# An attention and two-MLP kernel on one core: pieces of the written opening put in another order, zero products by a table

## The chip, the cores and the metric

The program runs on one core of a Trainium2 chip. The metric is device time in microseconds (us) of one execution; of several runs the median counts. The profile is one profiled execution. Its engines are PE (TensorE, matrix products; PEld is its weight load), DVE (VectorE), ACT (ScalarE), POOL (GpSimd) and SP (SyncE, which issues most DMAs). Every engine carries out its instructions in the order in which they are written.

## The reference, cut to what matters

Three layers follow one another on 4 x 768 = 3072 tokens of width 512: chunked attention with 8 heads and 8 memory keys, then an MLP with softplus, then an MLP with a leaky ReLU.

```python
attn_out = _attn_ref(q, k, v, mem_k, mem_v)         # chunks of 32, context 16 left, 8 right
x = attn_out.transpose(0, 2, 1, 3).reshape(3072, 512)
h = x @ moe_w_in                                    # 512 x 2048
x = (maximum(h, 0) + log1p(exp(-abs(h)))) @ moe_w_out
h = x @ moe2_w_in
return (maximum(h, 0) + alpha * minimum(h, 0)) @ moe2_w_out
```

The weights come as 64-bit floats, which the kernel turns into 32-bit ones by integer operations on DVE.

## The kernel before, in words

**Tiles.** Attention works on 24 tiles t of 128 tokens (4 make a block of 512). The first MLP runs over steps i = (block b, column group f of 128): `h.i` is PE's twelve products of x with the first weights, `out.i` the twelve products of the result with the second weights, summed over f in four banks of a block. Every operand is split in a high and a low part (three products instead of one). SEGMENTS begins with (block 0, f 0 to 3), (block 1, f 0 to 3), (block 0, f 4 to 7), (block 1, f 4 to 7): steps h.0 to h.3, h.4 to h.7, and so on, so h.4 to h.7 use the weights of h.0 to h.3 again. The second MLP follows in `pairs`, which the change does not touch.

**Pieces.** The opening and the first MLP are cut into pieces, added in `schedule`. Names used below:
- loads, issued by SP and moved by the DMA: `qk.t` (three DMAs: two halves of the queries, then the keys), `v.t` (six DMAs), `cst`, and `raw.n`, the n-th weight half of 128 x 512 64-bit words (`load_raw`). The halves k come in the order 0, 2, 1, 4, 3, 6, 5, 8, 7, ...; an even k = 2f is the first weight of f, an odd k its second.
- per weight half, on DVE: `ab` (`magnitude`), `cl` (`clamp`), `ca`, `cb`, `cv` (`convert_a` to `convert_c`); `wh` on ACT and `wl` on POOL split it in high and low.
- per attention tile: `qz` (POOL; DVE for tile 0) clears the half of the query tile that stays zero, `qo` and `qp` (ACT) place the queries, `km` (POOL) the memory keys; `s` (PE) scores, `m` and `c` (DVE) maximum and subtraction, `e` (ACT) exp, `n` and `r` (DVE) sum and reciprocal, `w` (POOL) the product with it, `t` (PE) transposes, `pt` (ACT) copies them, `v*` (PE) the values, `xh` (ACT) and `xl` (DVE) the split into x.
- per step: `h` (PE), `sp` (ACT softplus), `hi` (ACT), `lo` (DVE), `out` (PE). After the last step of a segment `dr` copies the four banks and `dd` stores them.

**Order.** `Plan.run` simulates the pieces greedily, with assumed durations and due times from the table O, eight times over, and the plan with the earliest end is taken; its `order` is then written out piece by piece. `InOrder` (line 71 is its call in the profile, so all rows have that line) ties each engine's instructions to that order. Rooms limit it: three raw buffers (`rpool`), three words, sixteen weight or tile rooms (`wpool`), two buffers each of ta and g.

**Zero products.** `keep_busy(name, ps)` writes `spare[name]` products with a zero operand ahead of a piece, into the bank that the piece then overwrites. Before, `spare` follows from the waits that the plan itself expects:

```python
    for name, (since, until) in plan.idle.items():
        if since > 0.0:
            spare[name] = max(0, int((until - since - 0.5) * 0.6 / 0.22))
        else:
            spare[name] = 8 + int((until - since - 7.0) * 0.6 / 0.22)
    for piece in plan.order:
        piece[4]()
```

By this the kernel before has 11 ahead of s.0, 9 of s.1, 2 of t.0, 3 each of t.1, v\*.1, v\*.2 and t.7, 4 each of v\*.3 and v\*.6, and 1 of t.5.

Of the kernel before, what the change touches and what calls it, by code (L numbers as in the profile page):

```python
# [81 lines left out]
PLAN = []  # L82
RUNS = 8
O = {'qo': 19.43, 'km': 103.61, 's': 132.4, 'm': 86.98, 'c': -51.87, 'e': 175.6, 'n': -19.49, 'r': -46.35, 'w': -19.52, 't': 95.77, 'pt': 85.42, 'v': 4.11, 'xh': -85.13, 'xl': -37.52, 'first': 4.43, 'gap': 13.49, 'second': 13.8, 'gap2': 10.89, 'raw': 76.14, 'ab': -97.97, 'cl': -24.77, 'ca': -41.63, 'cb': -28.14, 'cc': -52.39, 'wh': 1.69, 'wl': -37.29, 'odd': 61.8, 'sp': 29.0, 'hi': -84.66, 'lo': 120.66, 'out': 14.22, 'wait': 0.06, 'sloads': 10.35, 'qo0': 31.77, 'qo1': 59.63, 'km0': 45.44, 'km1': -1.09, 's0': 33.53, 's1': 68.06, 'm0': 99.26, 'm1': -29.86, 'c0': 87.42, 'c1': 86.99, 'e0': -47.46, 'e1': 46.23, 'n0': 20.17, 'n1': -4.91, 'r0': 23.19, 'r1': -6.49, 'w0': -81.15, 'w1': -23.28, 't0': 107.79, 't1': -40.96, 'pt0': 0.74, 'pt1': -5.53, 'v0': -87.68, 'v1': 71.52, 'xh0': -18.53, 'xh1': -22.32, 'xl0': 2.53, 'xl1': 34.49, 'by0': 3.34, 'by1': 1.01, 'va': -80.0, 'vb': -248.8, 'vc': -188.24, 'vd': -121.62, 'ra': -92.44, 'rb': -99.39, 'rc': -59.46, 'wld': -3.93, 'dra': -16.84, 'qpd': -4.87, 'ca0': 0.43, 'ca1': -2.85}


class Plan:
# [9 lines left out]
    def add(self, name, engine, us, due, work, after=(), take=(), give=(), table=None):  # L97
        assert name not in self.pieces, name
        self.pieces[name] = (engine, us, due, work, after, take, give, table)
# [4 lines left out]
    def run(self):  # L104
# [10 lines left out]
        while left:  # L115
# [19 lines left out]
            if engine and engine != "DMA":  # L135
                near = [x for x in able if x[3] == engine and x[0] < t + O["wait"]]
                if engine == "PE" and self.beside(last_pe):
# [39 lines left out]
def attention_mlp_mlp_kernel(ctx: ExitStack, tc, qk, v, w1, w2, consts, out):  # L177
# [19 lines left out]
    pe, act, dve, pool, sp = (InOrder(tc, e) for e in (nc.tensor, nc.scalar, nc.vector, nc.gpsimd, nc.sync))  # L197
# [19 lines left out]
    def load_raw(layer, k):  # L217

        t = rpool.tile([P, DM], mybir.dt.uint64, tag="raw", name="raw")
        sp.dma_start(out=t, in_=(w1, w2)[layer][k // 2, k % 2])  # L220
        raws[layer, k] = t.bitcast(I32).rearrange("p (n two) -> p n two", two=2)

    def magnitude(layer, k):
        m = words[layer, k] = tpool.tile([P, DM], F32, tag="word", name="word", bufs=3)
        dve.tensor_scalar(
            out=m.bitcast(I32), in0=raws[layer, k][:, :, 1], scalar1=1, scalar2=1,
            op0=ALU.logical_shift_left, op1=ALU.logical_shift_right,
        )

    def clamp(layer, k, eng=None):  # L230
        m = words[layer, k]
        (eng or pool).tensor_scalar(out=m, in0=m, scalar1=DBL_LEAST, scalar2=DBL_MOST, op0=ALU.max, op1=ALU.min)
# [7 lines left out]
    def convert_a(layer, k):  # L240
        mi = words[layer, k].bitcast(I32)
        dve.tensor_scalar(
            out=mi, in0=mi, scalar1=3, scalar2=0x3FFFFFFF,
            op0=ALU.logical_shift_left, op1=ALU.bitwise_and,
        )

    def convert_b(layer, k):
        r, mi = raws[layer, k], words[layer, k].bitcast(I32)
        dve.scalar_tensor_tensor(
            out=mi, in0=r[:, :, 1], scalar=-0x40000000, in1=mi, op0=ALU.bitwise_and, op1=ALU.bitwise_or  # L250
        )
# [56 lines left out]
    pt = [tpool.tile([P, NPAIR, 2, D], F32, tag=tag, name="pt") for tag in ("tb", "tl")]  # L308
# [598 lines left out]
    def schedule(when):  # L907
# [8 lines left out]
        def dma(name, issue, move, due, work, after=(), take=(), give=(), eng="SP"):  # L916
            add(("i",) + name, eng, issue, due, work, after, take)
            add(("x",) + name, "DMA", move, due, nothing, [("i",) + name])
            add(name, "", 2.0, due, nothing, [("x",) + name], [], give)

        for n, k in enumerate(order):
            f = k // 2
            need = when[first_use[f]] + (O["odd"] if k % 2 else 0)
            dma(("raw", n), 0.45, 1.9, (O["ra"], O["rb"], O["rc"])[n] if n < 3 else need - O["raw"], lambda k=k: load_raw(0, k), [("i", "raw", n - 1)] if n else [("i", "qk", TB - 1, 2)], ["raw"])
            add(("ab", n), "DVE", 0.45, need - O["ab"], lambda k=k: magnitude(0, k), [("raw", n)] + ([("ab", n - 1)] if n else []), ["word"])
            add(("cl", n), "DVE", 0.46, need - O["cl"], lambda k=k: clamp(0, k, dve), [("ab", n)])
            add(("ca", n), "DVE", 0.47, need - O["ca"], lambda k=k: convert_a(0, k), [("cl", n)] + ([("cv", n - 1)] if n else []))
            add(("cb", n), "DVE", 0.71, need - O["cb"], lambda k=k: convert_b(0, k), [("ca", n)])
# [175 lines left out]
        when = came + [came[-1] + 2.72 * 2]  # L1104
    plan = min(plans, key=lambda x: x.done["out", last - 1])

    for name, (since, until) in plan.idle.items():
        if since > 0.0:
            spare[name] = max(0, int((until - since - 0.5) * 0.6 / 0.22))
        else:  # L1110
            spare[name] = 8 + int((until - since - 7.0) * 0.6 / 0.22)
# [69 lines left out]
```

## Time and profile before

| | |
|---|---|
| runs shown | 1091.04 us median of 3 (1089.97 to 1093.57) |
| the profiled execution's own time | 1090.53 us |
| its span, first to last instruction | 1088.6 us |
| PE busy | 1064.7 us (98%) |
| DVE busy | 715.6 us (66%) |
| ACT busy | 559.0 us (51%) |
| POOL busy | 231.2 us (21%) |

The time is 1.9 us more than the span. Busy shares are means over the whole span; the opening, some 7% of it, looks different from the rest. Matmul records overlap by about 0.15 us and a few are missing, so lengths of groups are taken from start to start.

### The profile page before, as it was taken

How to read it: one execution, taken by the hardware profiler on the slowest of the kernel's cores; microseconds unless marked ns; L12 is line 12 of the kernel's file. 1: busy time of each engine (PE TensorE's matmuls, PEld its weight loads, DVE VectorE, ACT ScalarE, POOL GpSimd, SP SyncE). 2: the span in 40 equal slices, each digit the busy share in tenths (PEclk: the TensorE clock that was granted, in tenths of full speed). 3: DMA queues.
4: the chain of work that ended last, by engine and by line, in shares of the span. 5: the costliest groups of instructions: out<-in, count | busy, mean ns of one | idle time of the engine just before them, and what ended most of it. 6: DMA issues, size and time to landing. Idle time of an engine off the chain costs nothing.

```text
span 1088.6 us, 16448 instructions
## 1 busy us (share of the span) xinstructions
PE 1064.7 (98%) x5999; PEld 873.6 (80%) x6003; DVE 715.6 (66%) x1150; ACT 559.0 (51%) x974; POOL 231.2 (21%) x281
## 2 busy tenths in 40 slices
PE   6789999999999999999999999999999999999998
PEld 4578878888888888888888888888888888888886
DVE  6789989566744554454358156678666779566976
ACT  5654335565553554353244355664555755456643
POOL 4434434334222332223233400000000000000000
PEclk9999999999999999999999999999999999999999
DMA  9955574658644565444356373799874999856904
GB/s 227 226 154 173 170 190 129 172 170 207 173 143 155 158 188 139 171 123 145 107 201 229 132 289 125 283 280 323 199 278 174 329 299 256 251 209 251 377 1 78
DMA packets 173840, 214.55 MB, mean 197 GB/s; under 512 B 96064, under 2 KB 125888, under 8 KB 166848
## 3 DMA queue, kind: packets, MB, share of 16 engines
q1 hardware_dynamic: 169456, 196.59, 56.7%
q0 software_dynamic: 4032, 16.78, 7.8%
q8 instruction: 48, 0.79, 0.3%
q14 instruction: 32, 0.26, 0.1%
q10 hardware_dynamic: 272, 0.13, 0.0%
HBM read 154.74 MB, written 46.14 MB: 185 GB/s over the span
## 4 chain that ended last, share of the span: by engine, by line
PE 91%; DVE 3%; DMA 2%; issue 1%; SPq 1%; ACT 1%; POOL 0%; DVEq 0%; ACTq 0%; POOLq 0%
PE ps_q L71 42%; PE ps_o L71 23%; PE ps_hh L71 22%; DVE word L71 2%; PE ps_x L71 2%; PE ps_s L71 2%; DMA raw<-in_w_dram 1%; PE ps_t L71 1%; DMA qk<-in_qk_dram 1%; SPq L71 1%; DMA v<-in_v_dram 0%; ACT pt L71 0%; DVE sm L71 0%; DVE o_sb L71 0%; DVE g L71 0%
## 5 line engine op out<-in xcount | busy, mean ns | idle before, releaser
L71 PE MATMUL ps_hh<-x,wsplit 128*128 128x512 f32 x1152 | 281.1, 393 | 0.3 <-DVE x L71 0.2
L71 PE MATMUL ps_o<-g,wsplit 128*128 128x512 f32 x1152 | 279.1, 391 | 0.8 <-ACT ta L71 0.7
L71 PEld LDWEIGHTS ps_o<-g,wsplit 128*128 128x128 f32 x1152 | 214.8, 188 | 46.5 <-ACT ta L71 1.1
L71 PEld LDWEIGHTS ps_hh<-x,wsplit 128*128 128x128 f32 x1152 | 215.3, 189 | 45.5 <-DVE x L71 0.5
L71 PE MATMUL ps_q<-g,wout 128*128 128x512 f32 x1008 | 229.3, 389 | 0.0
L71 PE MATMUL ps_q<-xop,win 128*128 128x512 f32 x1008 | 229.1, 389 | 0.0
L71 PEld LDWEIGHTS ps_q<-g,wout 128*128 128x128 f32 x1008 | 189.0, 188 | 39.8 <-ACT gb L71 0.5
L71 PEld LDWEIGHTS ps_q<-xop,win 128*128 128x128 f32 x1008 | 189.2, 188 | 39.3
L71 DVE TENSOR_TENSOR g<-ta,g 128x512 fp32r<-128x512 f32 x96 | 71.2, 742 | 132.0 <-ACT g L71 131.8
L71 ACT CAST g<-gb 128x512 fp32r<-128x512 f32 x168 | 100.9, 622 | 89.6 <-PE ps_q L71 64.2
L71 DVE TENSOR_TENSOR g<-gb,g 128x512 fp32r<-128x512 f32 x168 | 114.0, 686 | 35.5 <-ACT g L71 33.6
L71 ACT CAST g<-ta 128x512 fp32r<-128x512 f32 x96 | 59.6, 621 | 147.5 <-PE ps_o L71 147.3
L71 ACT ACTIVATE ta<-ps_hh 128x512 f32<-128x512 f32 x96 | 57.4, 598 | 106.4 <-PE ps_hh L71 106.0
L71 DVE SCALAR_TENSOR_TENSOR word<-raw,word 128x512 int32<-128x512 int32 x128 | 104.6, 818 | 2.5
L71 ACT ACTIVATE tp<-gb 128x512 f32<-128x512 f32 x48 | 30.4, 633 | 91.8 <-DVE gb L71 91.8
L71 POOL TENSOR_TENSOR wst<-wsum,wst 128x512 fp32r<-128x512 f32 x32 | 42.1, 1316 | 122.4 <-ACT wst L71 122.3
L71 DVE TENSOR_SCALAR word<-word 128x512 f32<-128x512 f32 (+1 forms) x128 | 66.1, 521 | 1.8
L71 POOL DMA_DIRECT2D gb<-gb x12 | 10.5, 872 | 264.2 <-DVE g L71 183.0
L71 POOL TENSOR_TENSOR wsplit<-word,wsplit 128x512 fp32r<-128x512 f32 x32 | 48.9, 1530 | 64.4 <-ACT wsplit L71 64.2
L71 DVE TENSOR_SCALAR word<-raw 128x512 int32<-128x512 int32 x64 | 38.1, 597 | 36.8 <-DMA raw<-in_w_dram 23.8
L71 DVE SCALAR_TENSOR_TENSOR gb<-gb,tp 128x512 f32<-128x512 f32 x48 | 33.2, 691 | 44.0 <-ACT tp L71 44.0
L71 POOL TENSOR_TENSOR wst<-word,wst 128x512 fp32r<-128x512 f32 (+1 forms) x32 | 36.6, 1145 | 113.4 <-ACT wst L71 113.4
(81 smaller groups left out, 926.0 us busy)
## 6 DMA issues: line engine op xcount, KB each, us to landing
wout<-out_ops SPq DMA_DIRECT2D x42, 1024.0 KB
raw<-in_w_dram SPq DMA_DIRECT2D x64, 512.0 KB
win<-in_ops SPq DMA_DIRECT2D x24, 1024.0 KB
win<-in_ops SPq DMA_DIRECT2D x24, 768.0 KB
out_ops<-wst SPq DMA_DIRECT2D x56, 256.0 KB
in_ops<-wst SPq DMA_DIRECT2D x24, 512.0 KB
gb<-gb POOLq DMA_DIRECT2D x12, 1024.0 KB, 13.3
v<-in_v_dram SPq DMA_DIRECT2D x48, 128.0 KB
```

Source lines behind the costliest of these rows:

```text
L71: i = getattr(self.engine, name)(*args, **kw)
```

## The change

A table LATER of 293 pairs is added. After the plan is chosen, each pair (name, other) takes the piece `name` out of the order and puts it back right behind `other`. A second table WAITS replaces the plan's own waits as the source of the zero products. Nothing that is computed changes.

```diff
+LATER = ((('i', 'qk', 1, 2), 'qzero'), (('x', 'qk', 0, 2), ('x', 'qk', 1, 2)), (('qo', 0), ('qp', 1)), (('qp', 0), ('qo', 0)), (('i', 'v', 0), ('i', 'raw', 2)), (('i', 'v', 1), ('i', 'v', 0)),
...
+(('qz', 7), ('vr', 7)), (('qz', 2), ('qz', 7)), (('qz', 3), ('qz', 2)), (('qz', 6), ('qz', 3)), (('qz', 5), ('qz', 6)), (('qz', 4), ('qz', 5)), (('km', 0), ('qz', 4)), (('s', 0), ('km', 0)),
...
+(('i', 'v', 5), ('i', 'raw', 5)), (('x', 'qk', 4, 2), ('x', 'raw', 4)), (('qk', 4, 2), ('x', 'qk', 4, 2)), (('km', 4), ('qk', 4, 2)), (('i', 'qk', 6, 2), ('i', 'raw', 6)),
...
+(('raw', 7), ('qk', 7, 2)), (('ab', 6), ('raw', 7)), (('cl', 5), ('ab', 6)), (('m', 4), ('cl', 5)), (('c', 4), ('ca', 5)), (('cl', 6), ('c', 4)), (('wh', 3), ('cb', 5)), (('e', 4), ('wh', 3)), (('sp', 0), ('e', 4)),
...
+(('hi', 10), ('hi', 11)), (('lo', 11), ('hi', 10)), (('lo', 10), ('lo', 11)), (('out', 10), ('lo', 10)), (('sp', 12), ('out', 10)))
+
+WAITS = {('s', 0): (0.0, 9.7), ('s', 3): (13.6, 14.8), ('t', 0): (15.9, 16.5), ('t', 1): (17.2, 19.0), ('v*', 0): (19.7, 21.8), ('v*', 1): (24.9, 26.8), ('v*', 3): (28.2, 30.0), ('s', 4): (32.9, 35.8), ('v*', 7): (70.2, 70.3)}
...
     plan = min(plans, key=lambda x: x.done["out", last - 1])
 
-    for name, (since, until) in plan.idle.items():
+    for name, other in LATER:
+        names = [piece[3] for piece in plan.order]
+        piece = plan.order.pop(names.index(name))
+        names.remove(name)
+        plan.order.insert(names.index(other) + 1, piece)
+    for name, (since, until) in WAITS.items():
         if since > 0.0:
             spare[name] = max(0, int((until - since - 0.5) * 0.6 / 0.22))
         else:
```

Carried out on the plan's order, the pairs give these orders per engine (the part that differs and that is spoken of; what follows is as before).

PE before: s.0 s.1 t.0 s.2 v\*.0 s.3 t.1 v\*.1 t.2 v\*.2 t.3 v\*.3 s.4 h.0 s.5 h.1 t.4 s.6 v\*.4 out.0 s.7 t.5 h.2 v\*.5 t.6 v\*.6 t.7 h.3 v\*.7 out.1 h.4 out.2 h.5 out.3, and so on in turn.
PE after: s.0 s.1 s.2 s.3 t.0 t.1 v\*.0 t.2 t.3 v\*.1 v\*.3 v\*.2 s.4 h.0 h.1 t.4 out.0 v\*.4 s.5 out.1 s.6 h.2 s.7 t.5 h.3 t.6 v\*.5 out.2 v\*.6 t.7 v\*.7 out.3 h.4 h.5 h.6 out.4 h.7 h.8 out.5 h.9 out.6 h.10 out.7 h.11 out.8 out.9.

DVE before, from m.4: m.4 cv.2 c.4 ab.3 n.4 cl.3 r.4 ca.3 m.5 cb.3 c.5 cv.3 lo.0 m.6 lo.1 c.6 ab.4 n.5 cl.4 r.5 n.6 ca.4 r.6 xl.4 m.7 cb.4 c.7 ab.5 cv.4 cl.5 n.7 ca.5 r.7 cb.5 ab.6.
DVE after, from ab.3: ab.3 cv.2 xl.1 cl.3 ca.3 cb.3 cv.3 ab.4 cl.4 xl.2 ca.4 cb.4 cv.4 xl.3 ab.5 ab.6 cl.5 m.4 ca.5 c.4 cl.6 cb.5 n.4 r.4 ab.7 cv.5 lo.0 cl.7 ca.6 cb.6 cv.6 ca.7 cb.7 cv.7 lo.1 m.5 c.5 xl.4 m.6 n.5 c.6 r.5 n.6 m.7 r.6 c.7 lo.2 ab.8 ab.9.

ACT after, from wh.4: wh.4 qo.4 qp.4 wh.3 e.4 sp.0 hi.0 wh.6 qo.5 sp.1 pt.4 qo.7 hi.1 qp.5 wh.5 wh.8 xh.4 qp.7 qo.6 qp.6 e.5 e.6 sp.2 hi.2 pt.5 sp.3 e.7 pt.6 xh.5 wh.7 hi.3 xh.6 pt.7. Before, e.4 is followed by sp.0 hi.0 qo.6 qp.6 sp.1 pt.4 hi.1 e.5 qo.7 e.6 ... e.7 sp.2.

POOL before: qzero km.0 km.1 qz.1 km.2 qz.2 w.0 km.3 qz.3. POOL after: qzero qz.7 qz.2 qz.3 qz.6 qz.5 qz.4 km.0 km.1 qz.1 km.2 km.3 w.0 w.1 w.2 w.3 wl.0 wl.2 wl.1 km.4 wl.4 wl.3 w.4.

SP before: qk.0 qk.1 cst qk.2 qk.3 v.0 raw.0 v.1 raw.1 v.2 raw.2 v.3 qk.4 v.4 qk.5 v.5 raw.3 qk.6 v.6 raw.4 qk.7 v.7 raw.5 q.8 (two) qk.8 raw.6 v.8 raw.7.
SP after: qk.1 qk.0 cst qk.2 qk.3 raw.0 raw.1 raw.2 v.0 v.1 v.3 v.2 qk.4 raw.3 v.4 raw.4 qk.5 raw.5 v.5 raw.6 qk.6 raw.7 v.6 qk.7 v.7 q.8 (two) qk.8 raw.8 raw.9 v.8.

## Rows read from the trace of the kernel before

**Rows 1.** Windows: us, busy time (instructions) of PE, PEld, DVE, ACT, POOL; clock, DMA share, GB/s.

```profile
400.00:1000.00 600.00, 599.97 (x2865) 496.31 (x2861) 369.64 (x574) 309.67 (x545) 77.19 (x84) 1.00 0.67 216
```

**Rows 2.** Timeline of PE in the opening: start, length, instructions merged, idle before and its releaser.

```profile
1.01 4.07 PE L71 MATMUL ps_s<-zero 128*128 128x512 bf16 x11 [1.01 <-POOL zero L71]
...
6.72 1.17 PE L71 MATMUL ps_s<-qk,v 128*64 128x64 f32 x32 [1.64 <-POOL qk L71]
...
44.85 0.94 PE L71 MATMUL ps_t<-cst,v 128*128 128x128 f32 x4 [2.94 <-POOL v L71]
...
73.87 2.88 PE L71 MATMUL ps_hh<-x,wsplit 128*128 128x512 f32 x12
76.59 2.88 PE L71 MATMUL ps_o<-g,wsplit 128*128 128x512 f32 x12
```

**Rows 3.** Timeline of POOL: one piece qz (four instructions), and km.7.

```profile
12.01 1.17 POOL L71 MEMSET v<- 64x256 f32 x4
...
51.37 0.45 POOL L71 COPY qk<-qk 128x32 f32<-128x32 f32 x2 [5.78 <-DMA qk<-in_qk_dram]
```

**Rows 4.** Windows of ten microseconds (columns as in rows 1).

```profile
0.00:10.00 10.00, 7.25 (x51) 3.22 (x52) 4.76 (x15) 3.40 (x5) 2.98 (x17) 1.00 0.76 170
10.00:20.00 10.00, 5.94 (x135) 4.89 (x137) 5.70 (x13) 6.66 (x13) 4.15 (x15) 1.00 1.11 263
20.00:30.00 10.00, 7.14 (x87) 4.34 (x86) 9.86 (x20) 5.50 (x13) 5.58 (x11) 1.00 0.95 248
30.00:40.00 10.00, 8.02 (x113) 6.28 (x114) 5.87 (x8) 7.92 (x14) 6.28 (x15) 1.00 0.74 194
40.00:50.00 10.00, 6.60 (x80) 5.42 (x79) 6.76 (x16) 6.61 (x13) 2.20 (x4) 0.83 1.12 256
50.00:60.00 10.00, 7.87 (x58) 6.28 (x58) 9.12 (x19) 5.78 (x11) 4.74 (x7) 0.83 1.02 246
```

**Rows 5.** DMA issues of the page: what, issuing engine, count, size of each.

```profile
raw<-in_w_dram SPq DMA_DIRECT2D x64, 512.0 KB
...
v<-in_v_dram SPq DMA_DIRECT2D x48, 128.0 KB
...
qk<-in_qk_dram SPq DMA_DIRECT2D x8, 320.0 KB
```

**Rows 6.** Groups by shape from 0 to 140 us: count, busy us, mean ns, idle before.

```profile
L71 DVE SCALAR_TENSOR_TENSOR word<-raw,word 128x512 int32<-128x512 int32 x47 | 45.0, 958 | 0.2
...
L71 DVE TENSOR_SCALAR word<-raw 128x512 int32<-128x512 int32 x25 | 16.8, 671 | 4.9 <-DMA raw<-in_w_dram 4.9
L71 DVE TENSOR_SCALAR word<-word 128x512 int32<-128x512 int32 x24 | 14.9, 623 | 0.2
...
L71 ACT COPY pt<-ps_t 64x256 f32<-64x256 f32 x32 | 11.7, 366 | 12.2 <-PE ps_t L71 11.5
L71 DVE TENSOR_TENSOR g<-ta,g 128x512 fp32r<-128x512 f32 x15 | 11.3, 754 | 1.6 <-ACT g L71 1.6
...
L71 DVE TENSOR_SCALAR word<-word 128x512 f32<-128x512 f32 x24 | 10.0, 415 | 0.0
...
L71 POOL TENSOR_TENSOR v<-v,r 128x512 f32<-128x512 f32 x8 | 8.8, 1104 | 13.3 <-DVE r L71 12.4 <-ACT pt L71 0.5 <-ACT v L71 0.3
...
L71 DVE TENSOR_REDUCE nm<-ps_s 128x8 f32<-128x512 f32 x8 | 5.5, 687 | 3.2 <-PE ps_s L71 3.1
...
L71 ACT ACT_TABLE_LOAD x4 | 5.1, 1283 | 0.8 <-PEq L1171 0.7
...
L71 DVE TENSOR_SCALAR sm<-sm 128x8 f32<-128x8 f32 x8 | 2.4, 297 | 0.0
...
L71 DVE RECIPROCAL r<-sm 128x8 f32<-128x8 f32 x8 | 1.6, 202 | 0.5
```

**Rows 7.** Timeline of DVE: ab.3.

```profile
41.93 0.43 DVE L71 TENSOR_SCALAR word<-raw 128x512 int32<-128x512 int32 x1 [4.47 <-DMA raw<-in_w_dram]
```

**Rows 8.** Windows of half a microsecond behind the wait for t.4 (columns as in rows 1).

```profile
45.50:46.00 0.50, 0.28 (x2) 0.00 (x0) 0.50 (x2) 0.18 (x1) 0.09 (x1) 0.50 1.00 262
```

1 line of the change is left out of this document (added).

## The prediction

> **What bounds the kernel now.** I read the windows first. From 400 to 1000 us TensorE (PE) is busy 599.97 of 600 us [rows 1]: nothing is left to win there, and every microsecond by which the opening ends later is a microsecond at the end. Then the timeline of PE. In the opening it is the other way round: PE stands still for 2.94 us before the transpose of attention tile 4, after POOL's product on v [rows 2]. The first point from which PE runs without a break is h.4, which starts at 73.87; the next group of twelve 512-column products follows after 76.59 - 73.87 = 2.72 us. By 73.87 PE has done 8 score pieces and 8 value pieces (about 1.15 us each, the length of s.0's row), 8 transposes (0.6) and 6 groups: 18.4 + 4.8 + 16.3 = 39.5 us of work, so 34.4 us of the opening are waits, zero products and slow clock [rows 2]. Only these can move. The new order has one group more (out.2) before v\*.7, so the sum compares like with like: before, that amount of work is done at 76.6, when out.2 starts; after, when v\*.7 ends.
>
> What the waits stand on is read from the windows by tens: from 10 us on the DMA moves 263, 248, 194, 256 and 246 GB/s, with its engines' share near 1 but for 30 to 40 [rows 4]. VectorE (DVE) waits too: 4.47 us for raw.3 before ab.3 [rows 7]. So the opening is a transfer queue first, and a DVE queue behind it.
>
> **The change part by part.** *POOL.* Six clearings qz move ahead of km.0. One takes 1.17 us [rows 3]; qzero ends about 2.0, so km.0 comes at 2.0 + 6 x 1.17 = 9.1 and s.0 at 9.5, where it started at 6.72 [rows 2]. Cover: s.3 needs tile 3's keys, the last of the four opening tiles, 2.4 MB, which by the rates are through about 13 to 14 whatever the order [rows 4]; t.0 and all later PE pieces stand behind s.3. Without that cover it would cost 2.8 us.
>
> *Zero products.* The formula under the table gives 15, 1, 0, 3, 4, 3, 3, 6 and 0 of them. Eleven took 4.07 us [rows 2], so 15 end by about 6.6, ahead of s.0; the six before s.4 (2.2 us at that pace) lie in the wait for tile 4's queries, which is longer. I cost them at nothing; if that wait closes, the six cost 2.2.
>
> *The loads.* raw.0 to raw.2 move ahead of the v loads, raw.3 to raw.7 ahead of v.4, qk.5, v.5, qk.6, v.6. A raw load is 512 KB; a v load is six parts of 16 to 128 KB, in all 512 KB; a qk load 320 KB of keys and 2 x 128 KB of queries [rows 5]: 0.524, 0.524 and 0.590 MB, issued by SP in one queue. By the rates, 1.70, 4.33, 6.81, 8.75, 11.31 and 13.77 MB have been moved by 10, 20, ... 60 us [rows 4]. In the new order raw.6 is complete after six qk, six v, seven raw and cst: 10.4 MB, by the count at 46.5; raw.7 after 11.5 MB, at 50.9. Two corrections: if the sag of 30 to 40 fills to its neighbours' 250, 0.56 MB more is through and raw.7 is in at 48.7; and a landing lags the count: tile 7's keys (8 qk, 7 v, 5 raw, cst: 11.1 MB, by the count 49.1) released km.7 at 51.37 [rows 3], 2.3 us behind. Bounds for raw.7: 48.7 and 53.2. I take 50.0 (sag filled, half the lag), and 45.6 for raw.6.
>
> *DVE.* This decides. Its new order is ... xl.3 ab.5 **ab.6** cl.5 m.4 ca.5 c.4 cl.6 cb.5 n.4 r.4 **ab.7** cv.5 lo.0 cl.7 ca.6 cb.6 cv.6 ca.7 cb.7 cv.7 **lo.1**. The first piece of raw.6 and that of raw.7 now stand ahead of tile 4's softmax and of both lo pieces that the out products need; as ab.3 did [rows 7], each holds everything behind it until its load lands. Before, ab.6 and ab.7 came after those. Prices are means of the opening, so POOL's interference is in them [rows 6]: ab 0.67, cl 0.42, ca 0.62, cb and cv 0.96, lo 0.75, m, n and c 0.69, r 0.30 + 0.20; successive pieces overlap by some 0.08. From 45.6: ab.6 to r.4, nine pieces, 5.7 - 0.6, end at 50.6; POOL's w.4 takes 1.10, so t.4 starts about 51.8, against 44.85 before [rows 2]. ab.7, cv.5 and lo.0 (2.4 - 0.2) end at 52.7, and out.0 starts at 52.8. Eight more pieces (6.25 - 0.64) end lo.1 at 58.3. PE meanwhile does out.0, v\*.4 and s.5 (5.0 us, to 57.8) and waits for lo.1. From out.1 at 58.4 the order out.1 s.6 h.2 s.7 t.5 h.3 t.6 v\*.5 out.2 v\*.6 t.7 v\*.7 is 4 x 2.72 + 2 x 1.15 + 3 x 1.15 + 3 x 0.6 = 18.4 us: 76.8. One wait stays in it: after v\*.6 ScalarE (ACT) does xh.6 (0.6) and pt.7 (4 x 0.366) [rows 6] while PE has only t.7, so v\*.7 starts 1.8 us late and ends at 78.6.
>
> *ACT.* e.4 stands ahead of sp.0, and exp and softplus alternate e.4, sp.0, e.5, sp.2, e.7, sp.4: five switches where there were three, at 1.28 us each [rows 6], 2.6 us more on ACT, hidden behind the DVE chain until e.7 (pt.6 still meets out.2's end). By the row nothing is added to the sum. The Trainium skill (ScalarE: Activation LUTs, What ACT_TABLE_LOAD costs) gives a switch 2.66 us, a drain included; by it pt.6 and v\*.6 would come 1.4 us later and the sum be 1.4 larger. The row shows the 1.28 alone.
>
> *Clock.* PE has nothing between h.1 (about 47) and t.4. Before, the idle stretch ahead of t.4 was followed by a granted clock of 0.50 at 45.5, that is 1.2 instead of 2.4 GHz [rows 8]. The same would stretch out.0 from 2.7 to at most 4.1; s.5 would end at 59.2 instead of 57.8. lo.1 covers that but for 0.8; I take nothing and keep 0.8 for the range.
>
> *After v\*.7* the order of out, h, hi and the drains changes as well. I cost it at nothing: h.4 to out.7 use the weights of h.0 to out.3 again, so the words that DVE prepares there are due only from h.8 on. If a lo piece came late there it would be once or twice half a group, up to 3 us.
>
> **Sum.** 78.6 - 76.6 = +2.0 us on the profiled execution's 1090.53: 1092.5. The median of the runs shown is 0.5 above that execution, so I give 1093.0.
>
> **Rivals.** *The queue carries more* (faster). If the raw loads land before DVE asks for them, ab.6 and ab.7 hold nothing, and DVE's own work bounds: with raw.4 in by 35, the seven pieces from ab.4 to xl.3 (5.0 - 0.5) end at 39.5, and the 21 from ab.5 to lo.1 take 15.0 - 1.6 = 13.4 more, so lo.1 ends at 52.9, 5.4 us earlier, and v\*.7 at 73.2: -3.4, so 1087.6. For it: the share of 0.74 from 30 to 40 [rows 4]. Against: no ten microseconds moved more than 263 GB/s, and at 263 from 20 us on raw.7 is still only in at 47.4. The Trainium skill (DMA: Bandwidth & Descriptors, Specifications) puts the limit of HBM at some 358 GB/s per core; by it raw.7 would be in about 40 and this case holds. The trace of before reaches 263 in its best ten microseconds here, so it speaks against counting on that.
>
> *The loads lag as tile 7's keys did* (slower). With the whole lag raw.6 lands at 48.9 and raw.7 at 53.2, and every microsecond past 45.6 goes through ab.6, ab.7 and lo.1 to v\*.7: +3.3, in all +5.3, so 1096.3. From raw.6 at 46.9 on it is slower by over 0.3%. For it: the 5.78 us that POOL waited for those keys [rows 3]. Against: SP, not only the engines, held loads back when the share was 0.74 [rows 4], and the new order claims the v and qk rooms earlier.
>
> **How the numbers follow.** 0.3% is 3.3 us, about what a measurement of this kernel can tell from no change: below 1087.8 is faster, above 1094.3 slower. Forecast 0.48, its own range 1091 to 1095: 0.39 within, 0.09 slower. More from the queue 0.28, 1085.0 to 1089.5: 0.20 faster, 0.08 within. Lag 0.24: 0.22 slower, 0.02 within. Faster 0.20, same 0.49, slower 0.31. The range reaches into both rivals: 1086.5 to 1097.5 leaves about a tenth at either end.
>
> **What would show it.** In the profile after: s.0 at about 9.5; ab.6 waiting for its raw load until about 45.6 and ab.7 ready near 50; t.4 near 51.8 behind 3 us or more of idle PE, with the granted clock at 0.50 behind it; out.0 at 52.8, out.1 released by lo.1 near 58.3; v\*.7 ending near 78.6; five table switches by h.4's softplus. It is wrong if raw.7 lands before 47, if DVE goes through ab.6 without waiting, if out.1 waits for something else than lo.1, or if PE stops again between 80 and 160 us by more than 1 us.

## The result, and the profile after

The changed kernel takes 1103.01 us (median of 6, 1101.47 to 1106.92) against 1091.57 us for the kernel before (6 runs beside it). The medians are 11.4 us apart; the ratio estimated from the runs is 1.0114, 95% interval 1.0098 to 1.0130, which is 12.4 us slower (10.7 to 14.2). The forecast was +2.0 us, the range reached to 1097.5. The profiled execution took 1103.32 us with a span of 1101.4, where the span before was 1088.6: +12.8.

The windows of the changed kernel (columns as in [rows 1]):

```profile
0.00:10.00 10.00, 6.70 (x33) 2.62 (x35) 3.26 (x12) 3.85 (x6) 8.91 (x38) 1.00 0.78 167
10.00:20.00 10.00, 8.42 (x134) 6.59 (x129) 8.33 (x21) 6.07 (x12) 3.82 (x11) 0.83 1.05 288
20.00:30.00 10.00, 5.21 (x81) 3.58 (x80) 9.90 (x17) 5.99 (x16) 5.00 (x4) 1.00 0.52 159
30.00:40.00 10.00, 3.92 (x65) 3.39 (x66) 4.36 (x7) 1.93 (x5) 1.96 (x4) 0.52 0.95 256
40.00:50.00 10.00, 9.14 (x59) 6.03 (x58) 5.99 (x12) 2.91 (x5) 2.63 (x2) 0.80 1.02 230
50.00:60.00 10.00, 5.87 (x18) 4.21 (x17) 9.21 (x18) 6.97 (x13) 4.03 (x6) 0.72 0.84 224
400.00:1000.00 600.00, 599.96 (x2898) 495.95 (x2897) 368.38 (x572) 308.53 (x543) 80.69 (x89) 1.00 0.67 215
```

The dense part is what it was [rows 1]; all of the loss lies in the opening. The sag that stood at 30 to 40 before [rows 4] has not filled: it stands at 20 to 30 and is deeper, 159 GB/s at a DMA share of 0.52. PE is then short of work until 43, at a granted clock of 0.52 from 30 to 40.

The timeline of PE in the changed kernel (columns as in [rows 2]):

```profile
9.44 4.69 PE L71 MATMUL ps_s<-qk,v 128*64 128x64 f32 x96 [2.30 <-POOL qk L71]
...
37.93 1.98 PE L71 MATMUL ps_x<-pt,v 128*64 128x64 f32 x32 [6.06 <-DVE x L71]
...
55.16 1.11 PE L71 MATMUL ps_t<-cst,v 128*128 128x128 f32 x4 [4.13 <-POOL v L71]
55.93 5.61 PE L71 MATMUL ps_o<-g,wsplit 128*128 128x512 f32 x12
...
63.48 3.02 PE L71 MATMUL ps_o<-g,wsplit 128*128 128x512 f32 x12
...
82.06 1.47 PE L71 MATMUL ps_x<-pt,v 128*64 128x64 f32 x32 [0.90 <-ACT pt L71]
83.46 3.01 PE L71 MATMUL ps_o<-g,wsplit 128*128 128x512 f32 x12
...
110.79 2.88 PE L71 MATMUL ps_hh<-x,wsplit 128*128 128x512 f32 x12
116.03 0.80 PE L71 MATMUL ps_o<-g,wsplit 128*128 128x512 f32 x1 [2.36 <-ACT g L71]
118.61 4.63 PE L71 MATMUL ps_o<-g,wsplit 128*128 128x512 f32 x11 [1.79 <-DVE g L71]
123.09 2.92 PE L71 MATMUL ps_hh<-x,wsplit 128*128 128x512 f32 x12
```

These are s.0; v\*.2; t.4 and out.0; out.1; v\*.7 and out.3; then h.10, out.7 in two parts, and h.11. Two blocks carry the loss:

1. **Up to v\*.7.** It ends at 83.46, where out.3 starts; the same amount of work was done at 76.6 before. That is +6.9, forecast was +2.0.
2. **out.7.** Without a stop h.11 would start 2 x 2.72 behind h.10, at 116.23. It starts at 123.09: +6.9. PE waits twice and does the eleven products behind the second wait in 4.5 us instead of 2.5.

Together 13.7; the kernel before has about 1 us of stops at out.8 and out.16 that this one has not, which leaves about the 12.8 of the spans.

Block 1 stands behind DVE, and DVE behind the raw loads. DVE's timeline, the first pieces on raw.3 (ab.3), raw.6 (ab.6) and raw.7 (ab.7):

```profile
36.25 0.43 DVE L71 TENSOR_SCALAR word<-raw 128x512 int32<-128x512 int32 x1 [5.58 <-DMA raw<-in_w_dram]
49.65 0.43 DVE L71 TENSOR_SCALAR word<-raw 128x512 int32<-128x512 int32 x1 [3.88 <-DMA raw<-in_w_dram]
54.57 0.82 DVE L71 TENSOR_SCALAR word<-raw 128x512 int32<-128x512 int32 x1 [0.65 <-DMA raw<-in_w_dram]
```

10.1 us of DVE go into these three waits. The chain of waits shows where the sag comes from (start, length, what):

```profile
10.93 8.85 DMA raw<-in_w_dram
19.79 0.31 SPq L71
```

SP had issued v.1's first part at 16.79 and issues the second when raw.2 has landed, at 19.79. raw.2 is the eighth DMA before it. The five issues ahead of that, from 12.62 to 16.79, fall in the same way within 0.02 us of the landing of the eighth before each: the loads of this program report on eight semaphores in turn. What follows, the rest of v.1, v.3 and v.2, is small parts of 0.3 to 0.6 us of SP each (one took 1.5). From 19.79 to 30.99 SP issues them and qk.4 one behind the other, with pauses of 0.04 to 0.12 us, and the eighth before each had landed half a microsecond or more earlier. So in the sag it is no longer the eight that hold the loads back but the time that SP takes to issue them: the six parts of v.4 (SP's timeline) take it 2.83 us for 512 KB, 185 GB/s at most. With raw.0 to raw.2 under way, from 14 to 17 us, the DMA had moved 411 GB/s (windows).

```profile
31.47 2.83 SPq L71 DMA_DIRECT2D v<-in_v_dram  x6
```

```profile
14.00:17.00 3.00, 2.17 (x42) 1.70 (x39) 2.97 (x8) 1.25 (x3) 1.40 (x3) 1.00 1.04 411
```

Block 2 is two in-order queues. ACT's timeline ahead of out.7 (wh.17, then hi.7), and DVE's (cb.18, then lo.7):

```profile
114.84 0.62 ACT L71 CAST wsplit<-word 128x512 fp32r<-128x512 f32 x1 [2.44 <-DVE word L71]
115.37 0.61 ACT L71 CAST g<-ta 128x512 fp32r<-128x512 f32 x1
```

```profile
117.27 0.69 DVE L71 SCALAR_TENSOR_TENSOR word<-raw,word 128x512 int32<-128x512 int32 x1
117.88 0.69 DVE L71 TENSOR_TENSOR g<-ta,g 128x512 fp32r<-128x512 f32 x1
```

hi.7 stands behind wh.17, which waits for DVE's words of a weight half (k = 17) that PE does not use before out.16, at 166.65; lo.7 stands behind five pieces of the next two halves. sp.7 had been done at 101.1. (wh and wl are numbered by the half k, raw and DVE's pieces by the place of the load: wh.8 is made of raw.7's words; from 15 on the two numbers are the same.)

### The profile page after: what moved, and what is told of

The parts are those of the page before. It is cut to its first block, busy times and chain, and to the rows that moved or that the text cites. A ratio compares the mean times of both kernels' runs of the same rounds, so it can differ in the third digit from the quotient of the medians.

```text
span 1101.4 us, 16436 instructions
## 1 busy us (share of the span) xinstructions
PE 1071.3 (97%) x5995; PEld 877.5 (80%) x5995; DVE 716.7 (65%) x1150; ACT 561.1 (51%) x976; POOL 231.3 (21%) x281
## 4 chain that ended last, share of the span: by engine, by line
PE 90%; DVE 4%; DMA 2%; SPq 2%; issue 1%; ACT 0%; POOL 0%; DVEq 0%; POOLq 0%
PE ps_q L71 42%; PE ps_o L71 23%; PE ps_hh L71 21%; DVE word L71 3%; DMA raw<-in_w_dram 2%; SPq L71 2%; PE ps_s L71 2%; PE ps_x L71 2%; PE ps_t L71 1%; DVE g L71 1%; DVE x L71 0%; DVE o_sb L71 0%; ACT pt L71 0%; DVE nm L71 0%; ACT x L71 0%
## 5 line engine op out<-in xcount | busy, mean ns | idle before, releaser
L71 PE MATMUL ps_o<-g,wsplit 128*128 128x512 f32 x1152 | 284.2, 396 | 4.1 <-ACT g L71 2.4
L71 PEld LDWEIGHTS ps_o<-g,wsplit 128*128 128x128 f32 x1152 | 217.7, 190 | 51.5 <-ACT g L71 2.8
L71 DVE SCALAR_TENSOR_TENSOR word<-raw,word 128x512 int32<-128x512 int32 x128 | 98.8, 773 | 2.8
L71 DVE TENSOR_SCALAR word<-word 128x512 f32<-128x512 f32 (+1 forms) x128 | 73.0, 576 | 1.8
```

The source lines that it names most:

```text
L71: i = getattr(self.engine, name)(*args, **kw)
```

## The experiments

Ratios are to the kernel before, on the same chip; 0.001 is 1.1 us. The changed kernel has 1.0114. Edits are further pairs (piece, place behind which it goes), carried out after LATER.

### The late part, half mended

```diff
+MORE = ((('hi', 7), ('wh', 13)), (('lo', 7), ('cv', 15)), (('lo', 8), ('ca', 17)), (('hi', 9), ('db', 7)), (('lo', 9), ('cv', 18)))
```

> The changed kernel, with only the late part mended: hi.7 and lo.7 go ahead of hi.8 and lo.8 (behind wh.13 on ACT, behind cv.15 on DVE), hi.9 and lo.9 ahead of wh.18 and behind cv.18. Theory: the second block of loss is the order of these pieces alone; out.7 then follows h.10 at once near 113.5 and h.11 starts near 116.3 instead of 123.09, so the whole takes 1103.0 - 6.9 = 1096.1, 0.4 per cent over the kernel before. Rival: out.7 is late because the opening is late as a whole (words not ready), so that the wait only moves to out.8 or out.9 and less than 2 us come back (1101 or more).

Measured: 1.0079 [1.0058, 1.0100]. out.7 now follows h.10 at once, but out.8 stops instead (PE's timeline):

```profile
114.14 2.88 PE L71 MATMUL ps_hh<-x,wsplit 128*128 128x512 f32 x12
118.77 1.66 PE L71 MATMUL ps_o<-g,wsplit 128*128 128x512 f32 x6 [1.75 <-ACT o_sb L71]
121.59 4.41 PE L71 MATMUL ps_o<-g,wsplit 128*128 128x512 f32 x18 [1.16 <-DVE o_sb L71]
```

The wait passed to the drains dr.7, which stand behind wh.18 and cv.19 in the two queues. Neither theory had it whole: order it is, but of more pieces than were moved.

### raw.6's and raw.7's pieces behind the softmax of tile 4

```diff
+MORE = ((('ab', 6), ('lo', 0)), (('cl', 6), ('ab', 6)), (('ab', 7), ('lo', 1)), (('cl', 7), ('ab', 7)), (('ca', 7), ('cl', 7)), (('cb', 7), ('ca', 7)), (('cv', 7), ('cb', 7)))
```

> The changed kernel, with ab.6 and cl.6 moved behind lo.0 on DVE, and ab.7, cl.7, ca.7, cb.7, cv.7 behind lo.1; loads, ACT, PE and POOL as in the changed kernel. Theory (DVE's written order: the first pieces on raw.6 and raw.7 hold tile 4's softmax and the lo pieces back): t.4 comes near 51.4 instead of 55.16, out.1 near 59 instead of 63.48, and about 4 us come back at the end: 1099, if the late part stays as it is. Rival (the transfers bound whatever DVE's order is): pieces behind the raw loads are late in the same measure, out.1 comes at 62 or later, and under 1.5 us come back: 1101.5 or more.

Measured: 1.0133 [1.0110, 1.0156], nothing gained. Half of the theory came nearly to the letter: t.4 at 51.86, and out.0 behind a wait of 1.14 instead of 4.13 us took 3.08 instead of 5.61. But s.5 waits 3.06 and s.6 2.94 us for ACT. PE's timeline, then ACT's (qo.7, with hi.1 and qp.5 behind it; wh.8, with qp.6 behind it):

```profile
51.86 0.66 PE L71 MATMUL ps_t<-cst,v 128*128 128x128 f32 x4 [1.14 <-POOL v L71]
52.27 3.08 PE L71 MATMUL ps_o<-g,wsplit 128*128 128x512 f32 x12
...
59.49 1.15 PE L71 MATMUL ps_s<-qk,v 128*64 128x64 f32 x32 [3.06 <-issue]
...
66.52 1.15 PE L71 MATMUL ps_s<-qk,v 128*64 128x64 f32 x32 [2.94 <-ACT v L71]
```

```profile
57.62 0.62 ACT L71 COPY v<-qk 64x512 f32<-64x512 f32 x1 [2.93 <-DMA qk<-in_qk_dram]
...
63.27 0.62 ACT L71 CAST wsplit<-word 128x512 fp32r<-128x512 f32 x1 [3.23 <-issue]
```

In the changed kernel qo.7 waits for nothing (59.14, right behind pt.4): the wait was there all along, under DVE's. The time is the rival's, but what held PE are qp.5 and qp.6, which stand on ACT behind pieces whose loads they do not need.

### The loads alone

SP's order becomes raw.0, v.0, raw.1, v.1, raw.2, v.3, qk.4, raw.3, v.2, v.4.

```diff
+MORE = ((('i', 'raw', 1), ('i', 'v', 0)), (('i', 'raw', 2), ('i', 'v', 1)), (('i', 'v', 2), ('i', 'raw', 3)))
```

> The changed kernel, with SP's queue alone altered: raw.0, v.0, raw.1, v.1, raw.2, v.3, qk.4, raw.3, v.2, v.4 ... where the changed kernel has raw.0, raw.1, raw.2, v.0, v.1, v.3, v.2, qk.4, raw.3, v.4. Theory (SP issues a load only when the eighth before it has landed, and 24 small parts of v one behind the other carry too few bytes): from 20 to 30 the queue moves 240 GB/s or more instead of 159, raw.3 lands near 31.5 instead of 36.15, DVE's wait before ab.3 falls from 5.6 to about 1, raw.6 comes 1 to 2 us earlier, and 1 to 2 us come back at the end: 1101 to 1102. Rival (what was lost from 20 to 30 comes from the transfers themselves, or raw.6 is bound by the sum of bytes alone): the rate from 20 to 30 stays under 200 GB/s or raw.6 still lands at 49.5, and the time stays at 1103.

Measured: 1.0102 [1.0081, 1.0123], not to be told from the changed kernel. The windows:

```profile
20.00:30.00 10.00, 5.35 (x77) 4.12 (x77) 8.82 (x18) 5.66 (x14) 4.40 (x4) 0.80 0.85 254
30.00:40.00 10.00, 5.88 (x80) 3.80 (x81) 6.18 (x8) 4.92 (x11) 3.97 (x5) 0.84 0.69 174
```

and DVE's waits for raw.3 and raw.6:

```profile
32.82 0.43 DVE L71 TENSOR_SCALAR word<-raw 128x512 int32<-128x512 int32 x1 [1.40 <-DMA raw<-in_w_dram]
...
49.68 0.43 DVE L71 TENSOR_SCALAR word<-raw 128x512 int32<-128x512 int32 x1 [3.80 <-DMA raw<-in_w_dram]
```

The first half of the theory holds in its number, though what paced the small parts in the changed kernel was SP's issuing and not the places among the eight: with one raw load between two v loads the sag of 20 to 30 is gone, and raw.3 is 3.4 us earlier. The rival's second half holds too: the twelve parts of v.2 and v.4 now follow one another from 26.5 to 35.3, the sag stands at 30 to 40, and raw.6 lands when it did.

### The zero products alone

```diff
+    spare.update({('s', 0): 11, ('s', 1): 9, ('s', 3): 0, ('t', 0): 2, ('t', 1): 3, ('v*', 0): 0, ('v*', 1): 3, ('v*', 2): 3, ('v*', 3): 4, ('s', 4): 0, ('t', 5): 1, ('v*', 6): 4, ('t', 7): 3, ('v*', 7): 0})
```

> The changed kernel's order with the kernel before's numbers of zero products (s.0 11, s.1 9, t.0 2, t.1 3, v*.1 3, v*.2 3, v*.3 4, t.5 1, v*.6 4, t.7 3, none elsewhere). Theory: the zero products cost and bring nothing, 1103 within 1.5 us. Rival: those that the change puts before s.4 and v*.0 hold the clock up; without them s.4 and h.0 start later or run at half clock, and the time is 1 to 3 us longer.

Measured: 1.0103 [1.0076, 1.0129]. They cost and bring nothing that can be measured; without the six before it s.4 starts at 43.23 instead of 43.01.

### DVE's and ACT's order together, then with the late part

```diff
+MORE = (
...
+(('qo', 7), ('xh', 4)), (('km', 6), ('wl', 5)), (('wh', 8), ('qp', 6)), (('wl', 8), ('wh', 8))
```

> The kernel of run e2_raw_behind (ab.6 and cl.6 behind lo.0, raw.7's pieces behind lo.1), where t.4 came 3.3 us earlier but s.5 and s.6 waited for ScalarE; now ACT's qo.7 goes behind xh.4 and wh.8 behind qp.6, and on POOL km.6 goes ahead of wl.8. Theory (in-order queues: in e2 ACT stood at qo.7 until tile 7's queries landed near 57.6, with hi.1 and qp.5 behind it, and at wh.8 until cv.7 with qp.6 behind it): s.5 follows v*.4 at about 56.4, out.1 starts near 57.5 and s.6 near 60.5 instead of 63.48 and 66.43 in the changed kernel, v*.7 ends near 77.5 to 78.5, and 5 to 6 us come back at the end: a ratio of 1.0055 to 1.0065 to the kernel before, where the changed kernel has 1.0114. Rival (the loads bind whatever the order): tile 6's and 7's keys and queries or raw.7 are late in the same measure, another piece stands in their place, and less than 2 us come back (ratio 1.0095 or more).

Measured: 1.0096 [1.0078, 1.0114]. out.1 starts at 58.91 and v\*.7 ends at 80.16, 3.3 us earlier than in the changed kernel; by the ratios 2 us of it reach the end, which is within their intervals. The rival's number. In this run raw.3 landed 1.3 us later than in the changed kernel (37.58), and so everything behind it. Then the late part as well, with the drains:

```diff
+(('hi', 7), ('wh', 13)), (('lo', 7), ('cv', 15)), (('lo', 8), ('ca', 17)), (('out', 7), ('lo', 8)), (('db', 7), ('out', 7)), (('hi', 9), ('wl', 17)), (('dr', 7, 0), ('hi', 9)), (('dr', 7, 2), ('dr', 7, 0)), (('dr', 7, 1), ('cl', 19)), (('dr', 7, 3), ('dr', 7, 1)), (('lo', 9), ('cv', 18))
```

> The kernel of e5_order with the late part mended as in e1_late, and with the drains dr.7 moved as well: out.7 and its drains ahead of wh.18 on ACT and behind cl.19 on DVE, since in e1 out.8 waited 4.1 us for them (two stops, 118.77 and 121.6). Theory: the whole second block of loss, 6.9 us, is the place of hi.7, lo.7 and dr.7 in the written order; with e5's gain the time comes to within 2 us of the kernel before (ratio 0.998 to 1.002), and PE runs from h.4 to out.9 without a stop of more than 0.5 us. Rival: with the opening 5 us earlier, the second layer's words become the bound (DVE's cv.16 to cv.18 take as long as before) and stops of 2 us or more come back between out.6 and out.10: ratio 1.004 or more.

Measured: 1.0024 [1.0012, 1.0036]. 7.9 us come back by this edit, and PE does not stop between out.3 at 79.09 and out.15.

### The late part alone

The same late edit on the changed kernel, its opening left as it is.

> The changed kernel with the late part alone mended in full, as in e6_order_late: hi.7 and lo.7 ahead of hi.8 and lo.8, hi.9 ahead of wh.18, lo.9 behind cv.18, and the drains dr.7 behind hi.9 on ACT and behind cl.19 on DVE; the opening is the changed kernel's. Theory: the order of these pieces is the whole of the second block; PE runs from out.3 to out.15 without a stop and 7 to 8 us come back: a ratio of 1.004 to 1.005, where the changed kernel has 1.0114. Rival: with the opening late, words or drains are late too and a stop of 2 us or more stays between out.6 and out.10: ratio 1.007 or more.

Measured: 1.0045 [1.0027, 1.0063], in the middle of what was expected. v\*.7 ends at 84.46 here, as late as ever, and PE's timeline around out.7 (h.10, out.7, h.11, then out.8 with out.9) has no stop:

```profile
111.82 2.88 PE L71 MATMUL ps_hh<-x,wsplit 128*128 128x512 f32 x12
114.54 2.88 PE L71 MATMUL ps_o<-g,wsplit 128*128 128x512 f32 x12
117.26 2.88 PE L71 MATMUL ps_hh<-x,wsplit 128*128 128x512 f32 x12
119.98 5.60 PE L71 MATMUL ps_o<-g,wsplit 128*128 128x512 f32 x24
```

So some 7.5 of the 12.4 us (5 to 10 by the two intervals) are the place of hi.7, lo.7, the drains dr.7 and the neighbours that moved with them.

### The clock ahead of out.0

```diff
+    spare.update({('t', 4): 16})
```

> The changed kernel with 16 zero products ahead of t.4, in the 4.1 us in which PE has nothing (0.22 us each at full clock, 3.5 us). Theory: they keep the granted clock at 1.00 there, out.0 takes 2.7 to 3.1 us instead of 5.6, s.5 ends before lo.1 does, out.1 starts when lo.1 ends (62.3 instead of 63.48): 1.1 us come back, ratio 1.0104. Rival: the clock falls in spite of them, or out.0 is stretched by something else (its own waits); the ratio stays at 1.0114.

Measured: 1.0125 [1.0104, 1.0146]. In the trace the theory holds: the sixteen end 0.35 us before t.4, out.0's products take 3.3 us without their wait for lo.0, and out.1 starts with lo.1's end (62.87; 63.00) where it was 1.25 behind it in the changed kernel. But raw.6 landed 0.8 us later in this run, and the time shows no gain: some 1.2 us are within the interval, and less than the landings of the loads differ by from run to run.

### All of it

Run e7 has the late part, e5's order and e3's loads.

> The kernel of e6_order_late with the loads of e3_loads (raw.0, v.0, raw.1, v.1, raw.2, v.3, qk.4, raw.3, v.2). In e3 raw.3 came 3.4 us earlier and s.4 with it, but ab.6 still stood until 49.7. Theory: with ab.6 out of the way of tile 4's softmax, the earlier s.4 now shows: t.4 1 to 2 us earlier than in e6 and the end up to 1.5 us earlier. Rival: the next load in DVE's order (raw.5, before cl.5 and m.4) takes ab.6's part, t.4 stays within 0.5 us of e6 and the time is that of e6.

Measured: 1.0015 [1.0000, 1.0031], the time of e6. s.4 came 2.2 us earlier (40.77), t.4 1.4 us later (53.59): h.0 and h.1 stood from 43.46 to 53.6, with waits for xl.2 and xl.3, which DVE had behind raw.4's pieces, and at half clock. The rival's time, through another piece than it named.

### How early the opening can end with the changed loads

Run e9 pulls what attention, h and out need ahead of the pieces on raw words; e10 is e9 with e3's loads.

```diff
+(('cv', 2), ('wl', 2)), (('xl', 1), ('cv', 2)), (('v*', 2), ('xl', 1)), (('wh', 1), ('v*', 2)), (('xh', 3), ('wh', 1)), (('xl', 3), ('xh', 3)), (('xh', 2), ('xl', 3)), (('xl', 2), ('xh', 2)), (('wl', 1), ('xl', 2)), (('h', 0), ('wl', 1)), (('qo', 4), ('xl', 2)), (('qp', 4), ('qo', 4)), (('s', 4), ('km', 4)), (('h', 1), ('s', 4)), (('m', 4), ('cl', 4)), (('c', 4), ('ca', 4)),
...
+(('lo', 0), ('pt', 4)), (('lo', 1), ('lo', 0)), (('out', 0), ('lo', 1)),
...
```

> The kernel of e6_order_late, with every piece that DVE, ACT and POOL do for attention and for h and out pulled ahead of the pieces that wait for a raw load: cv.2, xl.1, xl.3, xl.2 ahead of ab.3; qo.4, qp.4 ahead of wh.4; m.4, c.4 behind cl.4, n.4, r.4, lo.0, lo.1 ahead of ab.5; h.0 ahead of s.4; later pieces in the same manner. SP's order is that of the changed kernel. Theory: in the changed kernel's opening the loads bind PE only through DVE's and ACT's order, so with nothing behind a raw load that does not need it t.4 starts near 46 to 47 instead of 52.1 in e6, out.0 near 47, v*.7 ends at 73 to 75 instead of 79.2, and the end comes 4 to 6 us earlier than e6: a ratio of 0.997 to 0.9985 to the kernel before. Rival: the loads themselves bind (keys, queries and v of tiles 5 to 7 come in behind raw.3 to raw.7): s.5 to s.7 and v*.5 to v*.7 wait for their landings, v*.7 ends no earlier than 77.5 and the ratio stays at 1.001 or more.

> The kernel of e9_pull with the loads of e3_loads (raw.0, v.0, raw.1, v.1, raw.2, v.3, qk.4, raw.3, v.2). Theory: tile 4's keys and queries are issued 2 to 3 us earlier, s.4 and t.4 follow where they and not DVE bound, and the end is up to 1.5 us earlier than e9. Rival: h.0 and xl.2 bind t.4's neighbours, and v.2, now behind raw.3, makes v*.2 later by as much: the time of e9 within 1 us, or longer.

Measured: e9 1.0011 [1.0000, 1.0022], e10 1.0024 [1.0009, 1.0039] with t.4 at 47.74 instead of 48.10. t.4 gained 4.0 us on e6 and out.1 2.5 (55.05), but t.5, t.6, v\*.5 and t.7 waited 4.3 us in all, and v\*.7 ended at 79.69. Those waits were for c.6, w.6, pt.5 and w.7, behind raw.7's pieces and wh.8 in the queues (w.7 behind raw.8's and raw.9's on DVE); PE itself waited for no load. So e9's theory missed its time and the rival had the number without its reason. Four further runs each took away the stop that the last had shown:

```diff
+(('m', 4), ('cv', 3)), (('c', 4), ('m', 4)),
...
+(('ab', 7), ('ca', 9)), (('cl', 7), ('ab', 7)), (('ca', 7), ('cl', 7)), (('cb', 7), ('ca', 7)), (('cv', 7), ('cb', 7)), (('wh', 8), ('pt', 7)), (('wl', 8), ('wh', 8)),
...
+    spare.update({('s', 4): 0, ('t', 4): 8})
```

> The kernel of e9_pull, whose opening lost again between t.5 and v*.7 what it had won (out.1 at 55.05, 2.5 us ahead of e6, yet v*.7 ends at 79.8): t.5 waited for c.6 and t.6 and pt.5 for w.6 and sp.2, which stood behind raw.7's pieces, wl.8 and wh.8. Now raw.7's five pieces go behind r.7 on DVE, wh.8 and wl.8 behind pt.7 and wl.7, m.4 and c.4 ahead of ab.4, raw.8 and raw.9 ahead of tile 8's queries on SP; no zero products before s.4 (1.4 us on the path in e9), eight before t.4. raw.7's words are first used by h.8 at 96. Theory: t.4 near 46, out.0 near 47, out.1 at 52 to 53, v*.7 ends at 73 to 75.5 instead of 79.2 to 79.8, and the ratio to the kernel before is 0.996 to 0.999. Rival: the opening ends early, but PE stops for the words of h.8 to h.11 instead (raw.10 and all behind it are issued 5 us later): stops of more than 2 us between 90 and 125, ratio 1.000 or more.

Measured: 1.0030 [1.0018, 1.0042]; t.7 stands 5.3 us for xl.5, which the edit had left behind raw.7's pieces. Neither theory foresaw it: the stop is the edit's own. Here the loads were late as well, raw.3 at 39.47.

```diff
+(('xl', 5), ('ab', 9)), (('xl', 6), ('ca', 9)), (('lo', 3), ('xl', 6))
...
+    spare.update({('s', 4): 0, ('t', 4): 16})
```

> The kernel of e11_pull2 with xl.5 ahead of cl.9, xl.6 and lo.3 ahead of raw.7's pieces on DVE, and 16 zero products before t.4 instead of 8. In e11 t.7 stood 5.3 us for xl.5 (78.57 to 79.26, behind ab.7 to cv.7), and out.0 took 5.36 us at half clock after 3.5 us without work. Theory (the loads, in the changed order, do not bind; only the written order does): t.7 follows w.7 near 74, v*.7 ends at 75 to 77, out.0 takes 2.7 to 3.1 us, and the ratio to the kernel before is 0.997 to 0.9995. Rival (the loads bind): tile 7's keys and queries or raw.8 stand in place of xl.5, v*.7 ends at 78 or later, ratio 1.001 or more.

Measured: 1.0027 [1.0015, 1.0040]. PE's timeline: t.4, out.0; v\*.7; h.4 in two parts:

```profile
45.52 0.60 PE L71 MATMUL ps_t<-cst,v 128*128 128x128 f32 x4
45.87 3.02 PE L71 MATMUL ps_o<-g,wsplit 128*128 128x512 f32 x12
...
71.81 1.15 PE L71 MATMUL ps_x<-pt,v 128*64 128x64 f32 x32 [1.50 <-ACT pt L71]
72.89 3.02 PE L71 MATMUL ps_o<-g,wsplit 128*128 128x512 f32 x12
77.71 0.50 PE L71 MATMUL ps_hh<-x,wsplit 128*128 128x512 f32 x1 [1.80 <-ACT x L71]
80.30 9.84 PE L71 MATMUL ps_hh<-x,wsplit 128*128 128x512 f32 x35 [2.08 <-DVE x L71]
```

v\*.7 ends at 72.89, 3.7 us ahead of the 76.6 by which the kernel before had done as much work, with the loads of the changed kernel up to v.7: so those loads are not what made the opening late. The gain went into xh.7 and xl.7, which stood behind wh.10 and ca.10, and into half clock behind that stop.

```diff
+(('xh', 7), ('v*', 7)), (('xl', 7), ('ca', 7)), (('sp', 4), ('dr', 3, 0)), (('hi', 4), ('sp', 4)),
...
+(('lo', 4), ('ab', 12)), (('sp', 5), ('wh', 9)), (('hi', 5), ('sp', 5)), (('lo', 5), ('cb', 12)),
...
```

> The kernel of e13_pull3, with xh.7 behind pt.7 and xl.7 behind ca.7, and from h.4 to h.12 the sp and hi pieces on ACT, the lo pieces and the drains ahead of the word pieces (wh, ab, cv) that they do not need. Theory (only the written order binds): h.4 follows out.3 near 75.8 and PE runs without a stop of more than 1 us to out.15, 5 to 6 us ahead of e13 at h.12 (119.89), that is h.12 at 114 to 116 against 117.78 in the kernel before; ratio 0.9965 to 0.9990. Rival (DVE's words bind from 80 to 125): stops of 2 us or more stand before out.4 to out.10, h.12 is no earlier than 117.5 and the ratio is 1.000 or more.

Measured: 1.0035 [1.0024, 1.0047], the rival's time. But PE comes to h.12 at 116.13, nearly where the theory had it and 1.65 us ahead of the kernel before, and then meets hi.10, behind wh.19, which this edit had not moved:

```profile
122.14 5.89 PE L71 MATMUL ps_o<-g,wsplit 128*128 128x512 f32 x12 [3.13 <-ACT g L71]
```

```diff
+(('out', 8), ('h', 11)), (('sp', 11), ('out', 8)), (('hi', 10), ('sp', 11)), (('lo', 10), ('cv', 18)), (('out', 9), ('lo', 10)), (('hi', 11), ('wh', 18)), (('lo', 11), ('cb', 19))
```

> The kernel of e14_pull4 with sp.11 and hi.10 ahead of wh.18 on ACT, hi.11 ahead of wh.19, lo.10 behind cv.18 and lo.11 behind cb.19 on DVE. Theory: out.10 follows h.12 without a stop near 118.9, h.13 starts near 121.6 instead of 127.83, PE runs on to out.17, and 5 to 6 us come back against e14: a ratio of 0.9975 to 0.9995 to the kernel before. Rival: DVE's words for h.16 and later bind once the opening is 6 us earlier; stops of 2 us or more between out.10 and out.19 take the gain back, ratio 1.001 or more.

Measured: 1089.84 us against 1090.49, 0.9994 [0.9982, 1.0005], profiled span 1086.9. PE's timeline, h.12 and out.10, and DVE's, ab.3:

```profile
115.69 2.88 PE L71 MATMUL ps_hh<-x,wsplit 128*128 128x512 f32 x12
118.41 2.88 PE L71 MATMUL ps_o<-g,wsplit 128*128 128x512 f32 x12
```

```profile
36.24 0.43 DVE L71 TENSOR_SCALAR word<-raw 128x512 int32<-128x512 int32 x1 [0.82 <-DMA raw<-in_w_dram]
```

This is at the upper end of the range that was expected: level with the kernel before, by the two ratios 1.2% faster than the changed one, with its loads up to v.7 and its zero products but for s.4 and t.4. raw.3 lands as late as in the changed kernel (ab.3 at 36.24; 36.25), and v\*.7 ends at 73.14. Between this and e14 lies one stop of 3.1 us and the slow products behind it.

## Why the prediction was wrong, point by point

- **POOL's clearings**: right. s.0 at 9.44 (9.5), hidden as said.
- **DVE decides, in order, through ab.6 and ab.7**: right as the chain of the changed kernel. ab.6 and ab.7 waited for their loads, t.4 stood behind 4.13 us of idle PE, and from ab.6 on the chain took what was forecast: ab.6's start to lo.1's end 12.6 us (12.7), out.1's start to v\*.7's end 20.0 (20.2). The second agreement is partly luck: the four groups took 0.9 us more than counted, and v\*.7 waited 0.90 us where 1.8 were counted. Nor does DVE decide alone: with raw.6's and raw.7's pieces out of the way (e2) ACT held PE, and nothing was gained.
- **The loads**: the first failed step. "Sag filled, half the lag" gave 45.6 for raw.6; it landed at 49.6. The sag moved to 20 to 30 instead of filling. By the new windows 10.4 MB are through at 47.4, and the landing is 2.2 us behind that: the whole lag. Bytes were moved in the count, but not what keeps them flowing: with the raw loads in front SP waits for raw.2, and then has small parts alone to issue, which it cannot issue fast enough. The lag rival had the row right and 48.9. This term is 4.0 of the 4.9 us by which block 1 was missed.
- **Clock ahead of out.0**: mis-sized, 0.8 at most; out.0 took 2.8 us longer and out.1 started 1.25 behind lo.1's end. That is the rest of block 1's miss; with the clock held (e8) the 1.25 went from the trace, but no gain showed in the time.
- **ACT's switches**: right. A softplus came 1.31 us behind e.4's end (52.67 to 53.98), with the load of 1.28 in it, and v\*.6 followed out.2 without a stop. ACT's timeline, e.4, the table load and sp.0:

```profile
52.04 0.63 ACT L71 ACTIVATE v<-v 128x512 f32<-128x512 f32 x1 [6.55 <-DVE v L71]
52.69 1.28 ACT L71 ACT_TABLE_LOAD   x1
53.98 0.60 ACT L71 ACTIVATE ta<-ps_hh 128x512 f32<-128x512 f32 x1
```

  The Trainium skill's 2.66 per switch (ScalarE: Activation LUTs, What ACT_TABLE_LOAD costs) does not agree with this spacing.
- **The queue carries more**: did not happen. The best ten microseconds moved 288 GB/s. But from 14 to 17 us, with the three raw loads under way, it was 411: the DMA could carry more, and was not given it. The Trainium skill (DMA: Bandwidth & Descriptors, Specifications) has about 358 as the limit of a core; the 411 measured here are above that.
- **After v\*.7 "at nothing, up to 3 us"**: the second failed step, and the larger one. The argument was that DVE's words are due late; true, and beside the point. hi.7, lo.7 and dr.7 were put behind those words, and the order of ACT and DVE from v\*.7 on was not followed piece by piece as it was up to v\*.7. e12 measures that order at 7.5 us. The text's own sign of error, a stop of PE of over 1 us between 80 and 160, came true.
- **Zero products**: no cost seen, as said (e4, to within its interval of some 3 us).

What the runs settle: e12 the second block. For the first, e2, e5, e9 and e11 to e15 show that the raw loads are late but bind PE mainly through pieces that stand behind them without needing them; with these pulled forward, and raw.3 as late as ever, the opening ends 3.5 us ahead of the kernel before (e15). Not separated is how the opening's share of the time splits between DVE's and ACT's order, since mending either alone uncovers the other; nor why raw.3 was there for ab.3 anywhere from 34.8 (e1) to 37.6 us (e5) in kernels whose instructions up to it are the same.

## What to carry to other kernels

When pieces are moved on in-order engines, follow every queue to the last piece that moved, asking of each that waits which pieces behind it do not need what it waits for; here words due 50 us later cost 7 us because the next result was queued behind them. A wait that is removed shows the one beneath it (DVE's raw.6, then ACT's qo.7, then wh.8), so price the second before counting the first as gain. Changing the order of loads changes their rate, so a count of bytes at the old rate does not carry over; small ones spread between the large moved faster in e3, though the time did not show it.

## What the runs showed that had not been expected

- SP issued no load before the eighth ahead of it had landed, and mostly needed 0.3 to 0.6 us for each, large or small. Behind three raw loads (512 KB each) it had only parts of 16 to 128 KB to issue, and the DMA moved 159 GB/s; with raw and v in turn it moved 254 in the same ten microseconds (e3).
- With the same instructions up to it, raw.3 was there up to 2.8 us earlier or later from one run's trace to another's (34.8 in e1, 37.6 in e5); by one trace of each, two openings that differ by less are not to be told apart.
- A stop of 3.1 us cost about 6: out.10 behind it took 5.89 us, and h.13 started at 127.83 (e14) instead of 121.13 (e15), with h.12 only 0.44 apart. Sixteen zero products right up to t.4 kept out.0 at 3.02 us (e13), where it had taken 5.61.
